# Four of six block inverses: formed in place in SBUF instead of PSUM, on two engines instead of one

## The chip, the cores and the metric

The kernel runs on one core of a Trainium2 chip. A core has TensorE (PE in the profile; PEld is its weight load), VectorE (DVE), ScalarE (ACT), GpSimd (POOL) and SyncE (SP, which here only issues DMAs). The metric is the device time of one execution in microseconds, the median of several.

## The reference, cut to what matters

A DeltaNet attention block (4 batches, 8 heads, 768 tokens, 48 features) followed by a multiplicative feed-forward block on 3072 tokens:

```
state = 0
for t in range(768):
    y[t] = q[t] @ state
    state += beta[t] * outer(k_n[t], v[t] - state.T @ k_n[t])      # k_n: k divided by its norm
x = y, heads beside each other                                      # (3072, 384)
out = ((x @ w1) * (x @ w2) @ w3) @ w_out                            # d_ff = 1024
```

## The kernel before, in words

The recurrence is cut into 12 chunks of 64 tokens. Within a chunk it becomes a triangular system: with a strictly upper matrix U of scores, the kernel needs the inverse of (1 + U). U is cut into 32 x 32 blocks; the two diagonal blocks are inverted directly, and the off-diagonal corner follows from two products. Two chunks are inverted together: 2 chunks x 2 block places x 32 (batch, head) pairs = 128 blocks, one per partition, with the 32 x 32 elements of a block in the free dimension. So there are six inverses, j = 0 to 5, and inverse j serves the chunks 2j and 2j + 1.

The steps of one inverse are the generator `inverse(j)`, whose name in the list of steps is `Vj`. V0 and V1 (`TURNED`) come from SBUF by transposes and are not changed. For V2 to V5 the blocks go through DRAM: `to_blocks` (u) writes them to `Ud`, L503 loads them into the SBUF tile `Ub` (U in the code), and ScalarE writes the identity into V, a pair of PSUM banks taken with `two_banks()` (L509, L514). Then come 31 dependent steps of two VectorE instructions: a product of a column of V and a row of U into the SBUF tile `tb` (L534), and its subtraction from V in PSUM (L539). Two ScalarE copies (L548) bring V back to SBUF, and L552 stores it to `Vd`; `from_blocks` reads it from there as the first step of `corner` (e). While V is in work its pair of banks is held; the psW pool has two such pairs, so everything else that uses `two_banks()` (scores s, corner e, chain c, outputs y) takes turns on the other one.

The other parts that matter here, by their names in the list: `c` is the chain of three products per chunk that carries the state, `y` its outputs, `n` a scaling of v on GpSimd (L666), `g` and `N` squares and norms of k (L329, L345 to L358), `d` transposes on VectorE (L383), `s` scores with a mask on GpSimd (L452). In the feed-forward part the tokens come in six groups u of 512. For u = 1 to 5 the hidden layer is formed by `m` (`pair`), 20 additions of products on TensorE (L1091) per half with their evictions on ScalarE and VectorE, after sums of tokens (`G`) and of weights (`W`, `T`); then come sums of the results (`S`) and the last products `o` (L1263) with their results `x` (L1293). The elementwise sums and products of G, W, S and of three steps of m go through one helper (L200):

```
def alone(out, x, y, op):
    (dve if other else pool).tensor_tensor(out=out, in0=x, in1=y, op=op)
```

The order of all work is written out by hand: `ORDER` is a text of some 1700 names, and each name runs the next step of its generator. All instructions of one engine run in the order of this text. A mark (') behind a name sets `other`, so that `alone` takes VectorE instead of GpSimd, and `put` changes sides between ScalarE and VectorE.

Of the kernel before, what the change touches and what calls it, by code (L numbers as in the profile page):

```python
# [51 lines left out]
P35 P29 v2 V1 V1 y1 b3 b1 y1 P28 y1 P29 f6 b2 c1 P29 f6 P34 b1 V1 V1 V1 V1 P31 P27 P28 V1 V1 V1 a00
f6 b2 P34 a02 a02 a00 P27 P28 V1 d4 P35 V1 V1 d4 a01 P34 a01 V1 V1 V1 V1 V1 V1 P35 a04 P31 P33 v3
a04 P33 a05 a03 a03 a05 b7 b7 a06 b5 p4 k4 n3 n2 n2 P35 V1 P30 V1 V1 V1 e2 P32 c1 a06 P33 d4 P31 k5
b4 a07 c2 d4 e2 e2 b4 e3 e2 b5 e2 P33 a04 e3 e3 a07 e2 c2 p5 b4 e2 a05 e2 P30 P32 c2 e3 P31 g2 g2 g2
g2 g2 a05 P30 b6 b6 b4 c2 y2 g2 g2 g2 P32 g2 a07 d5 d5 P30 p5 P32 b2 c2 N2 W n3 y2 s4 c2 b0 s4 a04
k6 T a07 s4 T s4 s4 b2 s4 e3 W s4 e3 a00 N2 a02 b0 d5 a00 d5 s5 s5 s5 s5 s5 s5 u4 a01 a01 S0' u5 V2
a06 s5 a02 p6 v4 c3 e3 g3 T W W T b1 W b6 W W W g3 a06 c3 b1 b5 b5 b6 S0 V2 e3 c3 c3 V2 V2 V2 V2 V2
V2 V2 V2 V2 a03 a03 b3 y3 b7 b3 y3 V2 b7 S0 W d6 V2 V2 V2 y3 W V2 V2 oA0 S0 S0 S0 V2 V2 oD0 S0 S0
S0' V2 n4 oB0 W W S0 S0 S0 xA0 oA0 c3 xA0 xB0 V2 d6 G1' W G1 oB0 c3 c4 xA0 oC0 V2 V2 V2 V2 V2 xB0 V2  # L60
m10 W W m10 S0 xD0 S0' G1 G1 G1 m10 m10 m10 m10 m10 G1' m10 p6 v5 S0 n4 W W xC0 V2 V2 V2 V2 V2 xC0
xD0 S0' V2 V2 V2 W' m10 V2 V2 e4 oC0 m10 m10 m10 d6 xC0 G1' c4 G1 W G1' m10 m10 m10 m10 m10 m10 m10
m10 m10 m10 m10 m10 m10 k7 s4 G1' G1' W' m10 e4 m10 m10 m10 m10' m10 m10 e4 e4 m10 e4 m10 m10 m10 e4
xC0 d6 p7 m10 m10 m10 m10 m10 m10 m10 m11 c4 n5 g3 c4 G1 g3 s5 m10 g3 g3 g3 m10 g3 m11 m10 m10' g3
m11 y4 d7 m11 m11 m11 m11 m11 d7 m11 N3 e5 m11 s6 m11 m11 m11 m11 m11 m11 m11 y4 p7 s6 s6 e5 m11 m11
m11 m11 d7 m11 c4 c4 d7 e5 e5 m11 m11 m11 m11 s6 k8 v6 s7 s7 s7 m11 g4 s7 s7 s7 m11 m11 s7 s6 n5 s6
m11 m11 g4 m11 m11 u7 u6 s6 m11 c5 e5 m11 c5 V3 m11 m11 m11 e5 V3 m11 m11 m11 m11 m11 c5 m11 oA1 c5
p8 S1' g4 g4 m11 V3 m11 S1 S1 y5 xA1 y5 N3 V3 V3 V3 V3 V3 V3 V3 d8 m11 V3 y5 oD1 d8 S1 S1 S1 V3 V3
V3 oB1 V3 V3 oA1 xB1 xA1 v7 n6 V3 V3 V3 V3 V3 G2 S1 n7 xA1 p8 S1 G2 G2 G2 c5 k9 G2 oB1 V3 V3 xB1 xD1
oC1 V3 m20 m20 m20 m20 m20 m20 m20 G2 m20 V3 xC1 xC1 V3 V3 V3 V3 m20 oC1 m20 m20 V3 V3 V3 V3 V3 xD1  # L70
G2 G2' xC1 m20 m20 m20 m20 m20 m20 s6 G2' m20 m20 m20 m20 m20 g4 s7 G2' n6 V3 V3 V3 c5 e6 xC1 m20
m20 m20 m20 m20 m20 m20 m20 m20 m20 m20 m20 c6 m20 c6 G2 G2 e6 m20 m20 m20 m20 e6 m20 g4 m20 m20 m20
m21 e6 e6 e7 d8 g4 e6 g4 g4 m21 m20 d8 m20 m21 c6 c6 s8 N4 s8 m20 m20 m21 m21 m21 m21 m21 m21 y6 p9
d9 d9 p9 s8 m21 m21 m21 m21 m21 m21 c6 y6 e7 m21 m21 m21 s8 m21 m21 c6 m21 s8 m21 s8 e7 d9 d9 m21 e7
m21 s8 m21 m21 m21' m21 s9 s9 m21 m21 n7 s9 s9 S2 s9 s9 m21 m21 u8 m21 m21 c7 m21 v8 m21 N4 m21 c7
s9 u9 V4 m21 m21 m21 m21 e7 e7 m21 m21 c7 c7 m21 m21 m21' S2 oA2 y7 oD2 S2 n8 S2 V4 V4 V4 V4 V4 V4
V4 V4 xA2 v9 V4 V4 V4 oB2 V4 V4 p10 d10 V4 S2 m21 n9 S2 xB2 oA2 V4 d10 y7 y7 oB2 V4 V4 V4 V4 G3 G3
G3 G3 G3 xB2 V4 V4 c7 xA2 p10 oC2 xA2 xD2 G3 m30 m30 m30 m30 m30 V4 V4 V4 V4 V4 xC2 n8 S2 G3 xC2 k10
S2 V4 V4 G3 G3 G3' V4 xD2 g5 s8 m30 m30 m30 m30 oC2 V4 V4 xC2 V4 V4 xC2 m30 m30 m30 m30 m30 m30 m30
m30 m30 m30 m30 m30 m30 V4 V4 c7 V4 m30 m30 m30 d10 m30 m30 m30 k11 m30 g5 G3 g5 m30 m30 e8 m30 m30  # L80
m30 c8 m30 m30 m31 g5 e8 c8 e8 m30 m30 m31 e8 m30 G3 m30 m30 e8 m30 n9 e9 e8 d10 s9 g5 g5 g5 g5 p11
m31 c8 m30 e9 m30 c8 y8 m30 e9 g5 e9 m30 N5 m30 m31 m31 m31 m31 m31 m31 m31 m31 d11 s10 d11 s10 p11
m31 m31 N5 m31 m31 s10 m31 m31 m31 m31 m31 m31 m31 c8 c8 y8 s10 s10 s10 s10 e9 m31 m31 m31 d11 d11
m31 e9 s11 s11 s11 s11 s11 s11 m31 m31 m31 m31 m31 m31 m31 m31 S3 c9 m31 c9 m31 m31 m31 m31 m31 m31
m31 s11 m31 u10 u11 V5 c9 c9 m31 V5 V5 y9 y9 y9 V5 V5 V5 oA3 m31 m31 S3 S3 oD3 S3 S3 m31 xA3 G4 V5
V5 V5 V5 V5 V5 V5 V5 V5 V5 G4 oB3 S3 oA3 S3 V5 V5 V5 V5 oC3 V5 xB3 V5 V5 V5 G4 G4 G4' V5 oB3 S3 xA3
xB3 xA3 G4 xD3 G4 G4 c9 V5 m40 m40 m40 m40 m40 m40 m40 m40 xC3 V5 V5 V5 V5 m40 V5 V5 m40 V5 V5 xC3
V5 V5 xD3 v10 n10 G4' oC3 c9 xC3 G4 V5 e10 v11 m40 m40 m40 m40 m40 m40 m40 m40 m40 m40 m40 m40 m40
m40 m40 m40 m40 m40 m40 s11 n10 m40 m40 m40 m40 G4 e10 c10 s10 e10 m40 m40 m40 G4 c10 m40 e10 m40
m40 m40 m40 m40 m40 e10 m41 m40 m41 m41 m41 e10 c10 e11 e11 m40 m40' m40' m41 m41 m41 m41 c10 c10  # L90
m41 e11 m41 m41 m41 c10 e11 m41 m41 m41 m41 m41 m41 m41 m41 m41 m41 m41 m41 m41 m41 m41 m41 m41 m41
n11 m41 m41 m41 m41 e11 c11 e11 m41 m41 m41 m41 m41 n11 c11 m41 m41 m41 c11 c11 y10 m41 m41 oA4 xA4
y10 y11 y11 m41 S4' m41' m41 S4' S4 S4 oD4 oB4 xB4 S4 oA4 S4 S4 oB4 xA4 y11 oC4 xB4 S4 G5' G5' G5 G5
xA4 xC3 xD4 xC4 xC4 G5' G5 m50 xD4 m50 m50 m50 m50 m50 m50 m50 m50 m50 m50 oC4 xC4 xC4 G5 G5' G5 G5
G5 G5 m50 m50 m50 m50 m50 m50 m50 m50 m50 m50 m50 m50 m50 m50 m50 m50 m50 m50 m50 m50 m50 m50 m50
m50 m50 m50 m50 m50 m50 m50 m50 m50 m51 m50 m50 m50' m50' m51 m51 m51 m51 m51 m51 m51 m51 m51 m51
m51 m51 m51 m51 m51 m51 m51 m51 m51 m51 m51 m51 m51 m51 m51 m51 m51 m51 m51 m51 m51 m51 m51 m51 m51
# [6 lines left out]
def kernel(  # L104
# [94 lines left out]
    def alone(out, x, y, op):  # L199
        (dve if other else pool).tensor_tensor(out=out, in0=x, in1=y, op=op)  # L200
# [297 lines left out]
    def inverse(j):  # L498
        U = in_turn(work, [P, BS, BS], "Ub", 1, "Ub")
        if j in TURNED:  # L500
            dve.transpose(out=U[:], in_=columns().rearrange("p t m g -> p t (m g)"))
# [7 lines left out]
        act.copy(  # L509
            out=flat[:, 0:n].rearrange("p (s t) -> p s t", t=BS + 1),  # L510
            in_=eye[:, 0 : BS + 1].unsqueeze(1).to_broadcast([P, BS - 1, BS + 1]),
# [948 lines left out]
```

## Time and profile before

| | |
|---|---|
| median of 3 runs | 568.31 us (566.58 to 569.11) |
| the profiled execution, its own time | 571.55 us |
| its span in the profile | 569.5 us |
| TensorE busy | 522.2 us |
| VectorE busy | 412.1 us |
| GpSimd busy | 269.6 us |
| ScalarE busy | 225.7 us |
| mean granted TensorE clock | 0.981 |

A row of groups in the profile reads: line, engine, operation, output <- inputs, shapes, count | busy us, mean ns of one | idle time of the engine just before, and what ended it. A row of the timeline reads: start in us, duration in us, engine, line, operation, shapes, count of merged instructions. A row of stretches reads: the stretch and its length, then the busy time of PE, PEld, DVE, ACT and POOL with the number of instructions in brackets, the granted clock, and the DMA share and rate. A row of waits reads: who waited, for whom, us in total, times, the longest.

### The profile page before, as it was taken

Reading aid. Unit: us, or ns where it says so; the run is one execution under the profiler, and the core shown is the slowest. Engines: PE = TensorE matmul, PEld = TensorE weight load, DVE = VectorE, ACT = ScalarE, POOL = GpSimd, SP = SyncE. Lnnn points to the kernel's source line nnn. Section 1 sums busy time; section 2 is a strip of 40 time slices with the busy share of each in tenths; the row PEclk is TensorE's granted clock in tenths of the full one; section 3 lists DMA queues with packets and bytes.
Section 4 is the critical chain, followed back from the end, with each engine's and each line's share of the span. In section 5 each row is a group of like instructions: output and inputs, shape, how many; then the busy total and the mean of one; then the engine's idle time right before and its main releaser. Section 6 shows DMA issues by size and latency. Waiting matters only on the chain.

```text
span 569.5 us, 19879 instructions
## 1 busy us (share of the span) xinstructions
PE 522.2 (92%) x8460; PEld 433.0 (76%) x8460; DVE 412.1 (72%) x881; ACT 225.7 (40%) x461; POOL 269.6 (47%) x287
## 2 busy tenths in 40 slices
...
GB/s 224 257 131 217 206 178 116 159 149 145 67 58 105 29 84 108 77 81 92 90 87 83 52 122 67 95 115 52 79 29 64 118 13 2 16 61 9 0 2 55
DMA packets 197591, 52.63 MB, mean 92 GB/s; under 512 B 184576, under 2 KB 191872, under 8 KB 197504
## 3 DMA queue, kind: packets, MB, share of 16 engines
...
q8 instruction: 66, 1.08, 0.8%
...
## 4 chain that ended last, share of the span: by engine, by line
PE 61%; DVE 20%; DMA 6%; issue 4%; SPq 3%; ACT 2%; POOL 1%; DVEq 0%; ACTq 0%; POOLq 0%
PE ps_f L1091 29%; PE ps_f L1263 13%; PE ps_w L680 4%; DMA raw<-in_moe_w_dram 3%; PE ps_w L779 3%; DVE tb L534 3%; PE ps_f L908 3%; DVE ps_w L539 2%; PE ps_w L609 2%; DVE ps_w L528 2%; DVE tb L523 2%; PE ps_w L432 2%; PE ps_w L426 2%; DVE ab L200 1%; DVE KQ L383 1%
## 5 line engine op out<-in xcount | busy, mean ns | idle before, releaser
L200 POOL TENSOR_TENSOR ab<-ab 128x512 f32<-128x512 f32 (+1 forms) x56 | 64.2, 1158 | 107.8 <-DVE ab L1170 66.4
L1263 PE MATMUL ps_f<-w,ab 128*128 128x192 f32 x376 | 65.3, 327 | 0.9 <-DVE ab L200 0.9
L1091 PE MATMUL ps_f<-xT,w1s 128*128 128x256 f32 x240 | 62.1, 390 | 2.6 <-DVE ab L1111 2.0
L1263 PEld LDWEIGHTS ps_f<-w,ab 128*128 128x128 f32 x376 | 61.8, 190 | 1.9 <-DVE ab L200 1.2
L1091 PE MATMUL ps_f<-xT,w2s 128*128 128x256 f32 x240 | 61.3, 388 | 1.6 <-DVE x_room L1108 0.7
L1108 DVE TENSOR_TENSOR ab<-ab,ps_f 128x512 f32<-128x512 f32 x60 | 41.0, 683 | 21.2 <-PE ps_f L1091 19.0
L1091 PEld LDWEIGHTS ps_f<-xT,w1s 128*128 128x128 f32 x240 | 42.6, 189 | 12.7 <-DVE ab L1108 2.5
L1091 PEld LDWEIGHTS ps_f<-xT,w2s 128*128 128x128 f32 x240 | 43.7, 190 | 10.7 <-issue 2.0
L1263 PE MATMUL ps_f<-room,ab 128*128 128x192 f32 x272 | 47.2, 329 | 4.0 <-DVE room L1293 2.8
L888 PE MATMUL ps_f<-w2s,w3T 128*128 128x384 f32 x128 | 45.9, 507 | 3.6 <-POOL w2s L837 3.0
L1263 PEld LDWEIGHTS ps_f<-room,ab 128*128 128x128 f32 x272 | 44.2, 190 | 5.1 <-DVE room L1293 2.4
L452 POOL TENSOR_TENSOR PT<-PT,smask 128x512 f32<-128x512 f32 x20 | 25.6, 1278 | 45.5 <-ACT PT L450 45.4
L539 DVE TENSOR_TENSOR ps_w<-ps_w,tb 128x31 f32<-128x31 f32 (+15 forms) x124 | 43.3, 349 | 4.5
L534 DVE TENSOR_TENSOR tb<-ps_w,Ub 128x31 f32<-128x31 f32 (+15 forms) x124 | 41.9, 338 | 4.8 <-DMA Ub<-Ud 1.7
L1091 PE MATMUL ps_f<-xT,room 128*128 128x256 f32 x160 | 41.7, 388 | 1.9 <-DVE osb L1293 1.9
L1102 ACT COPY ab<-ps_f 128x512 f32<-128x512 f32 x20 | 11.7, 585 | 72.9 <-PE ps_f L1091 67.5
L888 PEld LDWEIGHTS ps_f<-w2s,w3T 128*128 128x128 f32 x128 | 24.2, 196 | 19.9 <-POOL w2s L837 4.2
L798 ACT COPY xT<-ps_w 48x256 f32<-48x256 f32 x96 | 30.4, 365 | 16.6 <-PE ps_w L779 15.8
L1091 PEld LDWEIGHTS ps_f<-xT,room 128*128 128x128 f32 x160 | 29.0, 190 | 8.4 <-POOL xT L200 2.6
L426 PE MATMUL ps_w<-KQ 48*64 48x128 f32 x384 | 29.6, 299 | 5.5 <-DVE S L742 4.4
L432 PE MATMUL ps_w<-KQ 48*64 48x64 f32 x768 | 30.3, 235 | 2.9 <-issue 2.9
L1108 DVE TENSOR_TENSOR x_room<-x_room,ps_f 128x512 f32<-128x512 f32 x40 | 27.3, 683 | 6.6 <-PE ps_f L1091 5.9
...
## 6 DMA issues: line engine op xcount, KB each, us to landing
...
```

What stands on the lines that cost most here:

```text
L200: (dve if other else pool).tensor_tensor(out=out, in0=x, in1=y, op=op)
L426: pe.matmul(ps[half(z), 0, n : n + 128], lhsT=x[:, 0, :], rhs=x.rearrange("p j t -> p (j t)"), start=True, stop=True,)
L432: pe.matmul(ps[half(z ^ j), 1, n + C * j : n + C * j + C], lhsT=x[:, 0, :], rhs=x[:, j, :], start=True, stop=True,)
L452: pool.tensor_tensor(out=PT, in0=PT, in1=smask[:].unsqueeze(1).to_broadcast([P, H, C]), op=ALU.mult)
L534: dve.tensor_tensor(out=tv, in0=V[:, 0 : s + 1, s : s + 1].to_broadcast([P, s + 1, n]), in1=U[:, s, s + 1 : BS].unsqueeze(1).to_broadcast( ...
L539: dve.tensor_tensor(out=o, in0=o, in1=tv, op=ALU.subtract)
L680: pe.matmul(out(ps, r, h, z), lhsT=lhs(r, h, z), rhs=rhs(r, h, z), start=True, stop=True,)
L798: act.copy(out=xT[f, cc, p:NP:2, b : b + NR, :].rearrange("p a r t -> p r a t"), in_=pyv[f, z, b : b + NR],)
L888: pe.matmul(ps[:, 0:DM], lhsT=w3Ts[jc, kc // 4][:, kc % 4 * P : kc % 4 * P + P], rhs=wo[:, kc], start=(i == 0), stop=(i == KF - 1),)
L1091: pe.matmul(ps[:, n * g : n * g + n].rearrange("p (b c t) -> p b c t", b=HB, c=2), lhsT=product_weights(i, 2 * r + g), rhs=of[i], start=ne ...
L1108: dve.tensor_tensor(out=t, in0=t, in1=cell(name), op=ALU.add)
L1263: pe.matmul(ps[b][:, b, :], lhsT=block(u, HF * f + i, z)[:, P * b : P * b + P], rhs=ws_[w][:, i], start=first and i == 0 and (b == 0 or n ...
```

## The change

For j in 2 to 5 the inverse is formed in place in the SBUF tile `Ub`. ScalarE changes the sign of the whole tile, GpSimd sets everything on and below the diagonal to zero (`affine_select`), ScalarE writes ones on the diagonal. Then 30 steps follow, each with two instructions through `alone`: the product of a column and a row of U into `tb`, and its addition to U. No bank of PSUM is taken or held, and the tile is stored to `Vd` as it is.

```
+    ON_CHIP = (2, 3, 4, 5,)
...
+        if j in ON_CHIP:
+            flat = U[:].rearrange("p s t -> p (s t)")
+            act.mul(out=flat, in_=flat, mul=-1.0)
+            yield
+            pool.affine_select(
+                out=U[:], in_=U[:], pattern=[[-1, BS], [1, BS]], compare_op=ALU.is_gt,
+                fill=0.0, base=0, channel_multiplier=0,
+            )
+            yield
+            act.copy(
+                out=flat[:, 0 : BS * BS : BS + 1], in_=eye[:, 0:1].to_broadcast([P, BS])
+            )
+            yield
+            for s in range(1, BS - 1):
+                n = BS - 1 - s
+                t = in_turn(work, [P, 256], "tb", 2, "tb")
+                tv = t[:, 0 : s * n].rearrange("p (r t) -> p r t", t=n)
+                alone(
+                    tv, U[:, 0:s, s : s + 1].to_broadcast([P, s, n]),
+                    U[:, s, s + 1 : BS].unsqueeze(1).to_broadcast([P, s, n]), ALU.mult,
+                )
+                o = U[:, 0:s, s + 1 : BS]
+                alone(o, o, tv, ALU.add)
+                yield
+            Vds[j] = in_turn(dram, [P, BS, BS], "Vd", 2, "Vd")
+            sync.dma_start(out=Vds[j][:], in_=U[:])
+            yield
+            return
```

`ORDER` is new from its tenth line on (the start, up to about the first transposes of w3, is as before). Each of V2 to V5 has 35 names instead of 37. The marks that put a step on VectorE, counted over the whole list:

| steps | marked before | marked after |
|---|---|---|
| V2, V3, V4, V5 (30 arithmetic steps each) | (always VectorE) | 26, 25, 25, 22 |
| S, all groups | 14 | 28 |
| G, all groups | 16 | 27 |
| W | 2 | 10 |
| m, all | 11 | 15 |
| f4, t12 | 0, 0 | 1, 1 |

As an example of how the steps lie, the new list around V3:

```
m11 c5 m11 m11 m11 c5 oA1 m11 m11 c5 V3 xA1 g4 m11 g4 V3 v7 p8 V3 g4 m11' V3' V3' V3' V3' S1 V3' V3'
V3' V3' V3' V3' V3' V3' V3' V3' V3' c5 y5 m11 c5 oD1 y5 oA1 S1 S1 oB1 xB1 S1 S1 n6 oC1 y5 V3 d8 V3'
V3' V3' d8 G2 xA1 oB1 k9 xA1 G2' xB1 G2' G2' xD1 xC1 m20 S1' n6 S1 G2' V3 G2 V3 G2' c6 m20 m20 m20
m20 p8 m20 m20 m20 V3' V3' V3' V3' V3' V3' xC1 G2' G2 V3 m20 V3' V3 V3 xD1 oC1 e6 g4 m20 m20 m20
```

More of the change, by code (lines that the diff above doesn't have):

```diff
@@ L52 @@
[L52 to L97, printed above, removed]
@@ new lines @@
+t13 y1 b3 P28 P28 V1 V1 V1 V1 V1 V1 V1 y1 f6 P34 P30 b0 f6 f6 P28 c1 b0 P30 P33 b7 V1 V1 y1 p4 b2 b2
+b7 a05 a06 P30 V1 V1 V1 P33 a06 a05 V1 c1 a03 V1 V1 P34 P35 a04 b6 P33 a03 d4 P34 V1 V1 P30 P34 b6
+a04 P35 d4 V1 P35 P31 P31 P35 V1 V1 P31 V1 V1 V1 V1 V1 a00 c2 P32 a01 b4 v2 a02 N1 a01 a02 P31 b4
+P32 P32 b5 a00 b5 n2 b4 a06 P32 b1 V1 e2 e2 e2 k4 n2 g2 b4 e2 b3 e2 p4 e3 c2 a00 g2 g2 g2 a06 e2 e2
+e2 a02 d4 b3 b1 d4 W W' W' c2 b0 b2 k5 c2 b0 c2 b2 e3 g2 g2 g2 W e3 v3 p5 y2 g2 c2 e3 a00 a02 g2 y2
@@ new lines @@
+s4 b6 a01 a05 a04 d5 d5 N2 s4 s4 T N2 T T n3 W' s4 k6 e3 b6 s4 a01 n3 g3 a05 W' W a07 b7 p5 v4 W' e3
+s4 s4 d5 d5 c3 c3 n4 s5 s5 s5 a07 s5 n4 s5 a04 e3 e3 s5 b5 W W' b7 u4 u5 V2 s5 a07 c3 V2 p6 a03 a07
+W b5 c3 a03 T S0' S0' S0' W' W' S0' y3 y3 y3 W' g3 oA0 oD0 xA0 V2 S0' S0' V2 V2' V2 d6 S0' V2' c3
+S0' S0' S0' S0' V2 V2' V2' V2' S0 V2 oB0 c3 xB0 V2' V2' V2' oA0 xA0 k7 oB0 G1' V2' V2' S0 V2' xA0 v5
+G1' oC0 V2' xB0 G1 G1 s4 S0 G1 G1' xD0 S0' d6 m10 m10 m10 m10 m10 m10 m10 V2 V2' xC0 W V2' xC0 W'
@@ new lines @@
+V2' V2' V2' m10 m10 V2' G1' V2' G1' m10 S0 W V2' V2' V2' V2' V2' V2' V2' oC0 xD0 m10 m10 m10 m10 m10
+m10 m10 xC0 m10 W W W s5 G1 m10 m10 m10 m10 m10 m10 g3 G1 G1 p6 V2 m10 d6 m10 xC0 m10 m10 G1 n5 m10
+m10 m10 m10 g3 g3 m10 m10 e4 c4 m10 m10 m10 e4 c4 m10 d6 m10 m10 g3 g3 e4 e4 m10 m10 m10 m11 e4 m10
+m10 g3 e4 g3 m11 m11 c4 c4 p7 N3 m11 y4 m10 n5 m10 m11 m11 m11 m11 d7 d7 e5 p7 c4 k8 v6 m11 m11 m11
+m11 m11 m11 m11 m11 m11 e5 c4 m11 m11 m11 m11 m11 N3 y4 s6 s6 s6 e5 m11 d7 d7 m11 e5 m11 s7 s7 m11
@@ new lines @@
+s7 s7 s7 s7 s7 s6 m11 m11 m11 g4 s6 s6 u7 u6 V3 m11' m11 m11 m11 m11 S1' s6 e5 e5 c5 m11 m11 m11 m11
+m11 c5 m11 m11 m11 c5 oA1 m11 m11 c5 V3 xA1 g4 m11 g4 V3 v7 p8 V3 g4 m11' V3' V3' V3' V3' S1 V3' V3'
+V3' V3' V3' V3' V3' V3' V3' V3' V3' c5 y5 m11 c5 oD1 y5 oA1 S1 S1 oB1 xB1 S1 S1 n6 oC1 y5 V3 d8 V3'
+V3' V3' d8 G2 xA1 oB1 k9 xA1 G2' xB1 G2' G2' xD1 xC1 m20 S1' n6 S1 G2' V3 G2 V3 G2' c6 m20 m20 m20
+m20 p8 m20 m20 m20 V3' V3' V3' V3' V3' V3' xC1 G2' G2 V3 m20 V3' V3 V3 xD1 oC1 e6 g4 m20 m20 m20 xC1
@@ new lines @@
+c7 oA2 p10 V4 xA2 S2' m21 m21 m21' S2' S2' S2' y7 y7 g5 V4 V4 V4 g5 V4' V4' v8 V4' V4' y7 c7 s9 g5
+V4' oB2 oD2 v9 g5 c7 V4 m21' V4 xB2 V4' d10 d10 oA2 V4' V4' V4' V4' V4' xA2 S2 S2 V4' oB2 k11 xA2
+oC2 xB2 xD2 G3 G3' m30 m30 G3 G3 G3 G3 m30 m30 p10 m30 n8 xC2 xC2 xD2 V4' V4' V4' m30 V4' G3 S2 m30
+m30 m30 V4' G3' G3' c8 S2 m30 m30 m30 m30 N4 m30 m30 V4' V4' V4' V4' G3 m30 V4' V4' V4' oC2 g5 V4'
+n9 V4 g5 g5 V4 xC2 m30 m30 m30 m30 m30 n8 G3 m30 m30 m30 m30 c8 G3' n9 V4 m30 m30 m30 m30 m30 m30
+m30 m30 m30 m30 m30 m30 m30 m30 m31 e8 m31 d10 d10 m30 e8 m30 g5 g5 m30 m30 e8 e8 m31 m30 m30 e8 e8
@@ new lines @@
+m31 s10 N5 s10 c8 m30 m30 m31 s10 s10 c8 p11 m31 m31 m31 m31 m31 e9 s10 s10 s10 y8 d11 d11 p11 m31
+m31 e9 m31 v10 m31 xC2 u10 m31 y8 e9 m31 m31 m31 m31 m31 m31 m31 c8 c8 d11 e9 e9 e9 d11 m31 m31 m31
+m31 m31 m31 m31 c9 s11 s10 m31 c9 s11 s11 s11 m31 m31 m31 m31 s11 s11 u11 V5 c9 m31 m31 m31 N5 s11
+m31 m31 m31 m31 m31 c9 m31 oA3 S3' m31 m31 m31' S3' y9 V5 y9 y9 S3 S3 m31' oD3 xA3 oB3 V5 V5 V5' V5'
+V5' V5' V5' oA3 s11 S3' S3 xB3 oB3 V5' V5' V5' V5' V5' V5' V5' xB3 xA3 v11 xA3 oC3 S3' S3 G4 G4' G4'
```

28 lines of the change are left out of this document (22 added, 6 removed).

## Prediction

> **What bounds the kernel now.** I read the page first: busy shares, then the chain that ended last.
>
> ```profile
> span 569.5 us, 19879 instructions
> PE 522.2 (92%) x8460; PEld 433.0 (76%) x8460; DVE 412.1 (72%) x881; ACT 225.7 (40%) x461; POOL 269.6 (47%) x287
> PE 61%; DVE 20%; DMA 6%; issue 4%; SPq 3%; ACT 2%; POOL 1%; DVEq 0%; ACTq 0%; POOLq 0%
> ```
>
> TensorE (PE) is idle for 569.5 - 522.2 = 47.3 us in all, and the change removes no matmul. A gain can only come out of those 47 us, and only out of the part that lies where the four changed inverses lie. So the second view is the table by stretches. The first four run from the first step of V2, V3, V4 and V5 to the first product of the corner that needs the result; the other four from the first to the last step of each.
>
> ```profile
> core 0: us, PE busy (x) PEld busy (x) DVE busy (x) ACT busy (x) POOL busy (x), PEclk, DMA share, GB/s
> 178.70:224.60 45.90, 40.77 (x450) 35.26 (x452) 42.66 (x95) 8.67 (x19) 32.34 (x39) 1.00 0.35 71
> 266.20:304.70 38.50, 36.80 (x396) 31.70 (x385) 34.21 (x85) 9.88 (x23) 24.14 (x25) 1.00 0.42 85
> 341.00:379.50 38.50, 38.38 (x445) 33.58 (x447) 34.62 (x87) 9.77 (x22) 25.71 (x28) 1.00 0.51 98
> 415.20:456.80 41.60, 41.48 (x522) 36.55 (x525) 34.67 (x86) 10.84 (x23) 24.31 (x25) 1.00 0.30 68
> 178.70:213.20 34.50, 30.34 (x399) 27.55 (x398) 32.61 (x79) 5.40 (x14) 28.92 (x36) 1.00 0.31 60
> 266.20:293.30 27.10, 25.39 (x286) 23.27 (x275) 24.70 (x70) 6.55 (x17) 20.22 (x21) 1.00 0.45 83
> 341.00:368.20 27.20, 27.08 (x327) 25.34 (x327) 25.09 (x72) 6.72 (x16) 18.59 (x20) 1.00 0.45 78
> 415.20:442.50 27.30, 27.18 (x330) 25.53 (x330) 24.76 (x71) 6.01 (x15) 16.29 (x16) 1.00 0.18 46
> ```
>
> Two things are to be seen. PE's idle time in the four long stretches is 5.1 + 1.7 + 0.1 + 0.1 = 7.0 us: that is all a better inverse can win there. And while an inverse runs, VectorE (DVE) is busy 91 to 95% of the time: it is as full as PE, and a few microseconds more on it make PE wait.
>
> **The arithmetic steps.** The old steps of V2 to V5 are these groups.
>
> ```profile
> L539 DVE TENSOR_TENSOR ps_w<-ps_w,tb 128x31 f32<-128x31 f32 (+15 forms) x124 | 43.3, 349 | 4.5
> L534 DVE TENSOR_TENSOR tb<-ps_w,Ub 128x31 f32<-128x31 f32 (+15 forms) x124 | 41.9, 338 | 4.8 <-DMA Ub<-Ud 1.7
> L539 DVE TENSOR_TENSOR ps_w<-ps_w,tb 128x255 f32<-128x255 f32 x8 | 3.5, 432 | 0.3
> L539 DVE TENSOR_TENSOR ps_w<-ps_w,tb 128x31 f32<-128x31 f32 x8 | 1.6, 199 | 0.6
> L200 DVE TENSOR_TENSOR ab<-ab 128x512 f32<-128x512 f32 x16 | 10.5, 688 | 1.5 <-PE ps_f L1263 1.3
> L200 POOL TENSOR_TENSOR ab<-ab 128x512 f32<-128x512 f32 x44 | 55.8, 1277 | 107.8 <-DVE ab L1170 66.4 <-DVE ab L1108 18.5 <-DVE ab L200 16.8
> L200 POOL TENSOR_TENSOR xT<-xT 128x256 f32<-128x256 f32 x36 | 26.2, 738 | 11.0 <-DVE xT L200 8.2 <-DMA xT<-xT 2.3
> ```
>
> DVE pays (432 - 199) / 224 = 1.04 ns per element and about 0.16 us per instruction, and 688 ns for 512 elements wholly in SBUF is on that line, so SBUF operands by themselves cost DVE nothing. GpSimd (POOL) pays (1277 - 738) / 256 = 2.1 ns per element and 0.2 us per instruction; below 256 elements this is an estimate from those two rows. An old inverse has 5456 elements in each of its two passes, a new one 4960 (s(31-s) for s = 1 to 30).
>
> In the new list a mark behind a step's name puts it on DVE. Of the 30 steps of V2, V3, V4 and V5, 26, 25, 25 and 22 are marked. On DVE: 196 instructions and 34,028 elements, 196 x 0.16 + 34.0 x 1.04 = 66.7 us, where 43.3 + 41.9 = 85.2 us go. On POOL: 44 instructions and 5,652 elements, 8.8 + 11.9 = 20.7 us. The steps depend on each other, so what counts for one inverse is the sum: about 21.9 us against 21.3. The chain gets no shorter.
>
> **Head and tail.** Three rows price them.
>
> ```profile
> L509 ACT COPY ps_w<-eye 128x1023 f32<-128x1023 f32 x6 | 6.1, 1024 | 6.0 <-DVE vtok L711 3.6 <-DVE X L720 2.3
> L548 ACT COPY Ub<-ps_w 128x512 f32<-128x512 f32 x8 | 4.3, 591 | 4.6 <-DVE ps_w L539 4.6
> 1.81 0.29 POOL L215 TENSOR_SCALAR_AFFINE_SELECT strict<-strict 128x128 f32<-128x128 f32 x1
> ```
>
> The identity written into PSUM (1.02 us on ScalarE) went beside the load; in its place the chain gets a sign change (1.0), a select of 1024 elements, and a small copy of the diagonal (some 0.2). The select is between 0.3 us (its own 128 elements) and 8 x 0.29 = 2.3; I take 1.3. The tail loses two copies, 1.2 us. Net +1.3 us per inverse, on ScalarE and POOL, which have room at the start; I count it at nothing where the load comes early, else 5 us for the four.
>
> **What else the list moves.** Steps of the slab sums, token sums, weight sums and products go from POOL to DVE: marks on S 14 to 28, G 16 to 27, W 2 to 10, m 11 to 15. On DVE that is 14 + 11 + 8 + 4 instructions, 19 of 256 elements at 0.41 and 18 of 512 at 0.69, plus two copies: 21.6 us. POOL loses 19 x 0.73 + 18 x 1.28 = 36.9. Without anything else DVE would come to 412.1 - 85.2 + 66.7 + 21.6 = 415 us, POOL to 270 + 21 + 5 - 37 = 259. Busy time hardly changes.
>
> **The cost that decides: two engines and one way into SBUF.** An old step has one operand in PSUM. A new one on DVE has both in SBUF. What such an instruction meets when POOL works shows in the timeline.
>
> ```profile
> 217.22 0.41 DVE L200 TENSOR_TENSOR xT<-xT 128x256 f32<-128x256 f32 x1
> 192.20 4.56 DVE L200 TENSOR_TENSOR ab<-ab 128x256 f32<-128x256 f32 x1
> 191.65 1.40 POOL L200 TENSOR_TENSOR room<-room,w1s 128x256 f32<-128x256 f32 x2
> 193.02 2.08 POOL L200 TENSOR_TENSOR ab<-ab 128x256 f32<-128x256 f32 x3
> 195.07 1.40 POOL L200 TENSOR_TENSOR w2s<-room,w2s 128x256 f32<-128x256 f32 x2
> 240.92 0.19 DVE L348 TENSOR_TENSOR nt<-nt,nr 128x32 f32<-128x32 f32 x1
> 151.57 0.93 DVE L348 TENSOR_TENSOR nt<-nt,seed 128x32 f32<-128x32 f32 x1
> 151.45 1.96 POOL L958 TENSOR_TENSOR room<-w 128x384 f32<-128x384 f32 x2
> ```
>
> The same 256 elements take 0.41 us alone and 4.56 us while POOL has a row of instructions: DVE ends when POOL's queue runs dry at 196.47. A 0.19 us instruction takes 0.93 beside POOL, one POOL instruction's length. In the same stretch the old steps of V2, with PSUM operands, keep their 0.4 us. The Trainium skill's page "SBUF — State Buffer" (§ SBUF: two separate sides) says that a VectorE instruction with two SBUF inputs and a GpSimd instruction that reads SBUF exclude each other, and that the loser blocks until the first is through. The rows agree, with one addition: 4.56 us spans several POOL instructions, so the loser can lose again.
>
> How much POOL work do the 196 instructions meet? Between the first and the last step of each inverse the new list has on POOL, its own V steps left out: for V2 four S0, three G1, two W, one s4, 8.9 us; for V3 six S1, one m11, three G2, two n6, 12.8; for V4 four S2, seven G3, three g5, two n, one s9, 15.6; for V5 two S3, six G4, two n10, one s11, 9.8; in all 47 us (n, g and s by the rows below).
>
> ```profile
> L666 POOL TENSOR_TENSOR vtok<-vtok,n 128x384 f32<-128x384 f32 x24 | 20.5, 863 | 16.0 <-DMA vtok<-in_v_dram 16.0
> L329 POOL TENSOR_TENSOR sq<-ktok 128x384 f32<-128x384 f32 x24 | 19.8, 832 | 23.8 <-DMA out_dram<-osb 12.5 <-DVE ss L331 4.5 <-DMA ktok<-in_k_dram 3.7
> L452 POOL TENSOR_TENSOR PT<-PT,smask 128x512 f32<-128x512 f32 x20 | 25.6, 1278 | 45.5 <-ACT PT L450 45.4
> ```
>
> The bounds are 0 (every POOL instruction falls while DVE reads PSUM or waits) and 47 (each stops DVE for its whole length). DVE's own time there is 70 to 80% SBUF-only, and for about a quarter of the chain the step is on POOL and DVE isn't stopped. 0.78 x 0.77 gives 0.6: 28 us, 7 per inverse.
>
> **What of it reaches the end.** PE goes on until the corner's product. By the two lists, PE's work from an inverse's first step to that product is 40.8, 34.6, 32.0 and 35.4 us before, and 32.0, 34.9, 36.5 and 33.1 after, summed with these durations (one addition of a product is four records, 0.93 us):
>
> ```profile
> 291.49 10.24 PE ps_f L1091 x44
> 288.89 2.60 PE ps_f L1263 x16
> 301.74 1.08 PE ps_w L680 x64
> 304.74 0.69 PE ps_w L609 x50
> ```
>
> DVE needs, between first and last step, its V steps, marked sums and five to nine other instructions, 27.3, 24.9, 26.6 and 21.7 us. With 3.9, 5.1, 3.8 and 7.1 us of V steps on POOL and 0.6 of the POOL work above, 36.5, 37.7, 39.8 and 34.7; the trace before has 34.5, 27.1, 27.2 and 27.3. From the last step to the product it takes 11.4, 11.4, 11.3 and 14.3 us before; I take 11. Against PE's work in the list, and 0, 2, 6 and 6 us by which PE did more than the list's share before, PE lacks 15.5, 11.8, 8 and 6.6 us, where it lacked 5.1, 1.7, 0.1 and 0.1: +35 us. This is too much, since DVE's other instructions (5.2, 5.2, 7.5 and 3.6 us) can run while POOL has a V step; the smaller of the two, inverse by inverse, is 3.9 + 5.1 + 3.8 + 3.6 = 16 us. That leaves +19. The pair of PSUM banks that V no longer holds gives the score, corner and chain products a second place; it can win back only idle time that is already in the 7 us, and the larger waits above take that away, so I count it at nothing.
>
> Sum: the profiled execution took 571.55 us (span 569.5); it would take 590.5. The median of the runs before, 568.31, is 3.2 lower, so I predict 587.
>
> **The rivals.** First, the waits hardly coincide, because POOL is idle for half of the time and its work slips to where DVE reads PSUM. Then the sum without blocking counts, 35 - 28 - 16 = -9, and PE's idle 7 us in the four stretches go, with the second PSUM place to help: 568.3 - 7 = 561. For it speaks that the list takes 37 us off POOL, and that V3' stands eleven times in a row with no POOL step between; against it that these rows are list order, not time. It decides if less than a fifth of the 47 us blocks. Second, full exclusion: all 47 us block, 0.4 x 47 = 19 more: +38, 606. A row of POOL instructions as at 191.65 speaks for it, the many gaps of POOL against it; it decides where POOL always has work when DVE reaches a step. The skill's rule named above, taken without a gap, is this case. Third, the 22 POOL steps stand in a queue that waits for DVE:
>
> ```profile
> POOL ab L200 <- DVE ab L1170: 66.4, 8, 18.9
> ```
>
> If one V step in each inverse lands behind such a wait of mean 66.4 / 8 = 8.3 us, that is +33 us, 601. The list puts those products mostly behind the inverse, which speaks against it. Fourth, blocked time and new room cancel: no change beyond 0.5% (2.8 us, about what a measurement of this kernel can tell from none).
>
> **How the numbers follow.** The forecast has 0.54; the first rival 0.22 (its gain is 7 us at most, so nearly all of it lies beyond 0.5%); full exclusion 0.10; the queue 0.07; no change 0.07. Slower: 0.54 + 0.10 + 0.07 = 0.71. The range goes from the first rival's 561, a little below, to full exclusion's 606: 560 to 606. The forecast's own range is 575 to 600.
>
> **What would show it.** Right: the new add and multiply on DVE average well over 0.34 us, with single ones of 1 us and more that end when a POOL instruction ends; DVE's busy time rises to 440 or more; PE's idle time in the four stretches goes from 7 to about 25 us, ended by the corner's inputs or by DVE. What would make it wrong: DVE's V steps keep 0.34 us on average, or they are stretched and PE stays busy all the same, because PE's order leaves more work between than I counted.

## Result and the profile after

The changed kernel takes 605.59 us (median of 4 runs, 602.73 to 608.57); the kernel before took 567.96 us (566.58 to 569.11) beside it. The ratio is 1.0664, 95% interval 1.0588 to 1.074: 37.6 us slower.

The page of the changed kernel, and two views by groups: the steps of V2 to V5 on DVE and on POOL.

```profile
span 606.7 us, 19888 instructions
PE 533.7 (88%) x8460; PEld 440.6 (73%) x8460; DVE 447.2 (74%) x872; ACT 221.1 (36%) x451; POOL 264.9 (44%) x294
```

```profile
L201 DVE TENSOR_TENSOR tb<-Ub 128x130 f32<-128x130 f32 (+14 forms) x98 | 49.2, 502 | 9.0 <-POOL Ub L511 4.0
L201 DVE TENSOR_TENSOR Ub<-Ub,tb 128x130 f32<-128x130 f32 (+14 forms) x98 | 48.5, 495 | 3.7 <-ACT Ub L516 0.2
```

```profile
L201 POOL TENSOR_TENSOR Ub<-Ub,tb 128x30 f32<-128x30 f32 (+11 forms) x22 | 11.4, 516 | 1.7
L201 POOL TENSOR_TENSOR tb<-Ub 128x30 f32<-128x30 f32 (+11 forms) x22 | 9.8, 444 | 41.9 <-DVE Ub L201 41.4
```

PE has the same 8460 matmuls. Its idle time rose from 47.3 to 606.7 - 533.7 = 73.0 us, and the same matmuls took 533.7 us instead of 522.2: 25.7 + 11.5 = 37.2 us, the whole loss between the two profiled executions. The mean granted clock fell from 0.981 to 0.961, which is about the same 2% by which the matmuls got longer. The 196 steps on DVE take 97.7 us; worked out without blocking they were 66.7. POOL's 44 take 21.2.

The stretches of the changed kernel, as in the prediction: four from the first step of an inverse to the first product of the corner, four from the first step to the last.

```profile
core 0: us, PE busy (x) PEld busy (x) DVE busy (x) ACT busy (x) POOL busy (x), PEclk, DMA share, GB/s
181.30:232.30 51.00, 39.78 (x295) 33.40 (x293) 45.98 (x89) 7.38 (x16) 26.89 (x32) 0.90 0.30 63
274.60:318.90 44.30, 35.08 (x228) 30.58 (x228) 40.96 (x78) 7.77 (x18) 23.00 (x27) 0.88 0.33 65
357.00:409.90 52.90, 44.19 (x442) 36.99 (x441) 46.59 (x88) 10.04 (x24) 26.58 (x32) 0.94 0.33 66
451.80:495.20 43.40, 37.99 (x296) 31.66 (x294) 37.47 (x72) 6.78 (x13) 22.43 (x32) 0.96 0.21 54
181.30:220.40 39.10, 28.54 (x195) 24.77 (x193) 36.99 (x75) 5.61 (x13) 22.06 (x26) 0.91 0.28 53
274.60:309.90 35.30, 26.08 (x187) 24.14 (x187) 33.60 (x67) 5.99 (x15) 18.10 (x22) 0.85 0.26 45
357.00:399.00 42.00, 34.16 (x401) 29.31 (x401) 38.28 (x75) 7.68 (x20) 21.83 (x28) 0.95 0.31 59
451.80:486.70 34.90, 30.30 (x205) 25.62 (x203) 31.11 (x63) 5.01 (x10) 17.60 (x28) 0.95 0.15 40
```

The four long stretches last 191.6 us, where they lasted 164.5, and PE is idle in them for 11.2 + 9.2 + 8.7 + 5.4 = 34.6 us (unrounded), where it was idle for 7.0. DVE is still busy about 90% of the time, and PE is busy for 157.0 us in them as before (157.4): the stretches got longer, and PE didn't get more to do. The clock column, 1.00 in all four before, is now 0.88 to 0.96.

One place shows the mechanism: V3's first steps in the timeline, DVE, then POOL, then PE.

```profile
274.60 1.24 DVE L201 TENSOR_TENSOR tb<-Ub 128x30 f32<-128x30 f32 x1 [1.61 <-POOL Ub L511]
275.88 1.19 DVE L201 TENSOR_TENSOR Ub<-Ub,tb 128x30 f32<-128x30 f32 x1
...
282.89 0.27 DVE L201 TENSOR_TENSOR Ub<-Ub,tb 128x108 f32<-128x108 f32 x1
...
292.78 0.55 DVE L1323 TENSOR_TENSOR room<-room,ps_f 128x384 f32<-128x384 f32 x1
```

```profile
274.53 1.27 POOL L201 TENSOR_TENSOR ab<-ab 128x512 f32<-128x512 f32 x1
275.76 1.27 POOL L201 TENSOR_TENSOR ab<-x_room,late 128x512 f32<-128x512 f32 x1
276.98 4.96 POOL L201 TENSOR_TENSOR ab<-ab 128x512 f32<-128x512 f32 x4
281.90 0.83 POOL L696 TENSOR_TENSOR vtok<-vtok,n 128x384 f32<-128x384 f32 x1
```

```profile
282.25 2.76 PE L1293 MATMUL ps_f<-w,ab 128*128 128x192 f32 x16
293.48 5.46 PE L1293 MATMUL ps_f<-room,ab 128*128 128x192 f32 x16 [8.47 <-POOL Ub L201]
```

POOL runs six slab sums and a token scaling without a gap, and DVE ends one V step per POOL instruction. From 282.9 a step of 108 elements takes 0.27 us. Behind the run of V steps stands L1323, which empties the PSUM bank that PE needs: PE waits 8.47 us. The releaser printed there (what ended the wait, by the profile) is a V step on POOL that ends at 293.43; PE reads nothing of it, and L1323 ends at 293.33. After the pause, 16 matmuls take 5.46 us where the 16 ahead of it took 2.76. PE's waits by line name the same kind of place elsewhere, an eviction (L1323) that stands in DVE's order behind other work:

```profile
PE ps_f L1121 <- DVE osb L1323: 10.0, 4, 4.2
PE ps_f L1293 <- POOL Ub L201: 8.5, 1, 8.5
```

### The profile page after: what moved, and what is told of

Read it like the earlier page. It is cut to its first block, busy times and chain, and to the rows that moved or that the text cites. A ratio compares the mean times of both kernels' runs of the same rounds, so it can differ in the third digit from the quotient of the medians.

```text
span 606.7 us, 19888 instructions
## 1 busy us (share of the span) xinstructions
PE 533.7 (88%) x8460; PEld 440.6 (73%) x8460; DVE 447.2 (74%) x872; ACT 221.1 (36%) x451; POOL 264.9 (44%) x294
## 5 line engine op out<-in xcount | busy, mean ns | idle before, releaser
L201 POOL TENSOR_TENSOR ab<-ab 128x512 f32<-128x512 f32 (+1 forms) x39 | 49.3, 1271 | 122.4 <-DVE ab L1200 76.4
L1121 PE MATMUL ps_f<-xT,w1s 128*128 128x256 f32 x240 | 66.2, 409 | 12.9 <-ACT ps_f L1166 6.0
L1293 PE MATMUL ps_f<-w,ab 128*128 128x192 f32 x376 | 65.3, 327 | 0.0
L1121 PE MATMUL ps_f<-xT,w2s 128*128 128x256 f32 x240 | 63.8, 400 | 0.9 <-DVE x_room L1138 0.5
L1121 PEld LDWEIGHTS ps_f<-xT,w1s 128*128 128x128 f32 x240 | 45.2, 199 | 25.9 <-ACT ps_f L1166 7.9
L1293 PEld LDWEIGHTS ps_f<-w,ab 128*128 128x128 f32 x376 | 61.8, 190 | 0.9 <-DVE ab L201 0.3
L1293 PE MATMUL ps_f<-room,ab 128*128 128x192 f32 x272 | 51.0, 343 | 11.9 <-POOL Ub L201 8.5
L1293 PEld LDWEIGHTS ps_f<-room,ab 128*128 128x128 f32 x272 | 46.4, 198 | 14.6 <-POOL Ub L201 8.7
L201 DVE TENSOR_TENSOR tb<-Ub 128x130 f32<-128x130 f32 (+14 forms) x98 | 49.2, 502 | 9.0 <-POOL Ub L511 4.0
L1121 PE MATMUL ps_f<-xT,room 128*128 128x256 f32 x160 | 45.0, 412 | 10.6 <-DVE osb L1323 6.9
L1121 PEld LDWEIGHTS ps_f<-xT,w2s 128*128 128x128 f32 x240 | 46.6, 200 | 9.9 <-ACT x_room L1132 1.5
L201 DVE TENSOR_TENSOR Ub<-Ub,tb 128x130 f32<-128x130 f32 (+14 forms) x98 | 48.5, 495 | 3.7 <-ACT Ub L516 0.2
L1132 ACT COPY ab<-ps_f 128x512 f32<-128x512 f32 x20 | 11.7, 586 | 97.7 <-PE ps_f L1121 97.5
L453 POOL TENSOR_TENSOR PT<-PT,smask 128x512 f32<-128x512 f32 x20 | 26.0, 1300 | 47.5 <-ACT PT L451 47.5
L828 ACT COPY xT<-ps_w 48x256 f32<-48x256 f32 x96 | 30.5, 366 | 11.0 <-PE ps_w L809 10.5
```

Source lines behind the costliest of these rows:

```text
L453: pool.tensor_tensor(out=PT, in0=PT, in1=smask[:].unsqueeze(1).to_broadcast([P, H, C]), op=ALU.mult)
L828: act.copy(out=xT[f, cc, p:NP:2, b : b + NR, :].rearrange("p a r t -> p r a t"), in_=pyv[f, z, b : b + NR],)
L1121: pe.matmul(ps[:, n * g : n * g + n].rearrange("p (b c t) -> p b c t", b=HB, c=2), lhsT=product_weights(i, 2 * r + g), rhs=of[i], start=ne ...
L1132: act.copy(out=t, in_=cell(name))
L1293: pe.matmul(ps[b][:, b, :], lhsT=block(u, HF * f + i, z)[:, P * b : P * b + P], rhs=ws_[w][:, i], start=first and i == 0 and (b == 0 or n ...
```

## Experiments

Every ratio is taken to the kernel before, run beside it on the same chip. These runs come from three chips, on which the kernel before took 570.12, 569.99 and 568.04 us; beside the changed kernel it took 567.96. A difference in us between two runs below can therefore be off by some 2 us.

**The old arithmetic in the new list.** All 31 steps in PSUM on DVE, with the pair of banks held again; the list of steps is the new one.

```
         if j in ON_CHIP:
-            flat = U[:].rearrange("p s t -> p (s t)")      # ... sign, select, ones,
-            for s in range(1, BS - 1):                     # ... 30 steps in U
+            V = two_banks().rearrange("p a (s t) -> p (a s) t", t=BS)
+            held.add(("w", turns["w"]))
+            ...                                            # the old identity, 31 steps, two copies
+            held.clear()
```

> The new list of steps with the old arithmetic: V2 to V5 are formed in a held pair of PSUM banks, all 31 steps on VectorE whatever their mark; everything else as in the changed kernel. Theory (the steps are slow because both operands are in SBUF beside GpSimd): their 248 VectorE instructions go back to about 0.34 us, 85 us in all, PE's idle time in the stretches beside the inverses falls by 15 us or more, and the time is 575 to 588 us. Rival (the new list itself is what costs: evictions that PE waits for stand behind long runs of V steps, and VectorE has more sums to do): 597 us or more, since VectorE has even more to do here.

```profile
L528 DVE TENSOR_TENSOR ps_w<-ps_w,tb 128x31 f32<-128x31 f32 (+15 forms) x124 | 43.3, 349 | 8.7 <-ACT ps_w L517 4.4
L523 DVE TENSOR_TENSOR tb<-ps_w,Ub 128x31 f32<-128x31 f32 (+15 forms) x124 | 41.9, 338 | 3.8 <-DMA Ub<-Ud 0.8
```

615.16 us, ratio 1.0794 (1.073 to 1.0858). The steps took their old 0.34 us beside the same POOL work, as the theory said, but the time was above both kernels. The theory took the held pair to cost nothing, and that is what fell. One wait of PE is the largest of all here:

```profile
PE ps_w L811 <- DVE S L774: 14.6, 1, 14.6
```

This run mixes the operands' place, the list and the held pair, so it does not rule out the rival, that the list costs, whose 597 us or more it meets. The third run below has the pair alone.

**The new arithmetic in the old list.** The new branch goes into the kernel before, with all 30 steps on DVE and the old `ORDER`.

```
-                alone(
+                dve.tensor_tensor(
...
-                alone(o, o, tv, ALU.add)
+                dve.tensor_tensor(out=o, in0=o, in1=tv, op=ALU.add)
```

> The old list of steps with the new arithmetic: V2 to V5 in place in SBUF, all 30 steps on VectorE; sums stay on GpSimd as in the kernel before. Theory (two SBUF operands beside GpSimd): 240 VectorE instructions that alone would take 80 us take 115 to 130 us (mean 0.48 to 0.54), and the time is 595 to 612 us. Rival (the new list costs, the place of the operands doesn't): mean 0.33 us and 566 to 575 us.

```profile
L523 DVE TENSOR_TENSOR tb<-Ub 128x30 f32<-128x30 f32 (+14 forms) x120 | 63.4, 529 | 17.0 <-POOL Ub L510 14.0
L528 DVE TENSOR_TENSOR Ub<-Ub,tb 128x30 f32<-128x30 f32 (+14 forms) x120 | 61.7, 514 | 7.1 <-ACT Ub L515 2.8
...
PE ps_f L1292 <- DVE room L1322: 33.0, 4, 11.2
```

626.19 us, 1.0993 (1.0946 to 1.1039). With the list unchanged, the new arithmetic takes the steps from 85.2 to 125.1 us, within the theory's 115 to 130, and the kernel is 56 us slower, more than the theory's bound of 612 allows. PE's largest wait is again for an eviction on DVE. The operands' place is not all that differs: the new head comes with it, and the first steps wait 14.0 us for its select (L510, the first row above), which has its place in GpSimd's order. How the 56 us divide is not shown. The new list wins back about 20 us of them; by which of its moves is not shown either.

**The held pair, alone.** The changed kernel takes and holds an unused pair during each inverse.

```
+            unused = two_banks()
+            act.copy(out=unused[:, 0, 0:32], in_=eye[:, 0:32])
+            held.add(("w", turns["w"]))
             for s in range(1, BS - 1):
...
+            act.copy(out=U[:, 0, 0:1], in_=unused[:, 0, 0:1])
+            held.clear()
```

> The changed kernel, but V2 to V5 take a pair of PSUM banks that they don't use and hold it until they are stored, as the kernel before did; two small copies on ScalarE per inverse are added. Theory (the second pair wins nothing that counts): within 3 us of the changed kernel. Rival (the freed pair is worth something, and the blocking costs more than the net change shows): slower than the changed kernel by 5 us or more.

```profile
292.17 1.11 PE L814 MATMUL ps_w<-KQ,S 48*48 48x64 f32 x32 [16.54 <-DVE S L777]
```

620.78 us, 1.0899 (1.0839 to 1.0959): 13 us (by the ratios) to 15 us above the changed kernel, where the theory allowed 3. One wait is as large as that: the outputs y5 need the one pair that is left, and the DVE instruction that reads it (S) stands in the queue behind V3's run. The old arithmetic in the new list had the same wait (14.6 us). So the new list does lean on the freed pair. Against this run, the old arithmetic in the new list is 5.6 us cheaper, with 124 steps on DVE where this one has 98. While the pair is held, then, the place of the operands makes little difference to the whole: PE waits for the pair instead.

**The held pair in the old list.** The same hold, added to the second experiment.

> The old list with the steps in place on VectorE, as before, but V2 to V5 hold a pair of PSUM banks that they don't use. Theory (the pair is worth something only to a list that was made for it): 623 to 630 us, as without the held pair (626). Rival (a second pair is worth 10 us or more in any list): 636 us or more.

626.01 us, 1.0984 (1.0954 to 1.1013), against 626.19: in the old list the freed pair is worth nothing. Of these two orders, only the new one uses it.

**POOL only writes.** While an inverse is in work, the unmarked sums of S, G, W and m on POOL become memsets of about the same length; V's own steps stay. It leaves those sums out.

```
     def alone(out, x, y, op):
+        if running_v and not own and not other:
+            w = out.shape[-1]
+            pool.memset(out, 0.0)
+            pool.memset(out, 0.0)
+            pool.memset(out[..., 0 : w // 4], 0.0)
+            return
```

> The changed kernel, in which the sums that GpSimd does between the first and the last step of V2 to V5 (S, G, W, m without a mark) are replaced by memsets of about the same length into the same tiles, so these sums are left out of the result. GpSimd is as busy and gates the same products, but reads nothing from SBUF. Theory (GpSimd's reads stop VectorE's second operand): V steps on VectorE fall from a mean of 0.50 to 0.34 to 0.39 us, the time to 575 to 590 us. Rival A (any GpSimd instruction stops them, or they are slow for another reason): mean 0.46 us or more, time 598 or more. Rival B (the steps get faster, but PE waits in line for other things all the same): mean under 0.40 us, time 598 or more.

```profile
L209 DVE TENSOR_TENSOR tb<-Ub 128x130 f32<-128x130 f32 (+14 forms) x98 | 39.2, 400 | 6.7 <-POOL Ub L519 2.4 <-POOL Ub L209 1.9
L209 DVE TENSOR_TENSOR Ub<-Ub,tb 128x130 f32<-128x130 f32 (+14 forms) x98 | 38.4, 391 | 3.7
```

587.9 us, 1.0302 (1.0247 to 1.0357). The steps fell from 97.7 to 77.6 us (mean 0.395, a hair above the theory's 0.39), and the kernel won some 18 us.

**POOL only writes, everywhere.** The squares (L330), the score mask (L453) and the scaling of v (L696) become memsets too.

```
+                if running_v:
+                    in_place_of(sq[:], False)
+                else:
                     pool.tensor_tensor(out=sq[:], in0=kt[:, r], in1=kt[:, r], op=ALU.mult)
```

> As the run with writes only, and now GpSimd's scalings of v, squares of k and score masks beside an inverse are also memsets of about their length, so all of GpSimd's work between first and last step of V2 to V5, the V steps apart, reads nothing; these results are left out. Theory: V steps on VectorE come down to what they take alone, a mean of 0.34 to 0.36 us, and the time to 578 to 586 us; what then remains over the kernel before, 8 to 16 us, is not blocking but the new list: evictions that PE needs stand behind runs of V steps, and PE's clock falls after its pauses. Rival: blocking was all of it: 575 us or less.

The page, the groups, the four long stretches, and the same two V3 steps beside POOL's memsets:

```profile
PE 520.6 (90%) x8460; PEld 431.2 (75%) x8460; DVE 417.7 (72%) x872; ACT 220.5 (38%) x451; POOL 260.6 (45%) x385
...
L213 DVE TENSOR_TENSOR Ub<-Ub,tb 128x130 f32<-128x130 f32 (+14 forms) x98 | 36.0, 367 | 4.3 <-ACT Ub L534 0.7
L213 DVE TENSOR_TENSOR tb<-Ub 128x130 f32<-128x130 f32 (+14 forms) x98 | 35.4, 361 | 8.6 <-POOL Ub L529 3.7 <-POOL Ub L213 2.5
```

```profile
182.30:227.60 45.30, 37.87 (x295) 32.27 (x294) 40.38 (x89) 7.36 (x16) 25.95 (x53) 0.92 0.33 70
269.10:304.90 35.80, 32.65 (x242) 28.01 (x233) 32.38 (x78) 7.80 (x18) 22.34 (x50) 1.00 0.41 80
343.60:387.60 44.00, 40.19 (x436) 34.15 (x434) 39.01 (x88) 9.92 (x24) 24.68 (x61) 1.00 0.39 79
429.70:467.20 37.50, 35.86 (x297) 30.60 (x295) 31.66 (x72) 6.80 (x13) 21.32 (x52) 1.00 0.25 63
```

```profile
269.18 0.19 DVE L213 TENSOR_TENSOR tb<-Ub 128x30 f32<-128x30 f32 x1 [1.31 <-POOL Ub L529]
269.40 0.19 DVE L213 TENSOR_TENSOR Ub<-Ub,tb 128x30 f32<-128x30 f32 x1
...
269.08 0.53 POOL L204 MEMSET ab<- 128x512 f32 x1
```

579.31 us, 1.0166 (1.0135 to 1.0198). POOL is as busy as before (260.6 against 264.9 us), the list is the same, and the steps take 0.364 us on average. The two steps that took 1.24 and 1.19 us beside POOL's sums take 0.19 beside its memsets. So POOL's reading is what stops them. The kernel's 26 us need not all be blocking, though: a memset has no inputs to wait for, so POOL can also start sooner than with the sum in whose place it stands. The Trainium skill's page "SBUF — State Buffer" (§ Who interferes with whom) has it that a VectorE instruction with two SBUF inputs contends with a GpSimd instruction that reads SBUF, and not with one that only writes; this run agrees.

It also says where most of the 37.6 us are. In the four long stretches, 162.6 us now stand against 191.6. PE's idle time in them fell from 34.6 to 16.0, its busy time from 157.0 to 146.6: 18.6 + 10.5 = 29 us, the difference of the two spans but for 1 us (606.7 - 578.7 = 28.0). What is left is 9.3 us over the kernel before. PE's idle time in the stretches is 16.0 where it was 7.0, so this rest lies in the same place: I put it down to the list, in which evictions stand behind runs of V steps. That is argued from the stretches, not shown by a run of its own; POOL's own V steps, which still read, are in it too.

**A pause filled.** Eight dummy matmuls (16 records in the profile) before the second oB1 of V3, into a pair of banks of their own, so that PE works through the 8.5 us pause.

```
-V3' V3' d8 G2 xA1 oB1 k9 ...
+V3' V3' d8 G2 xA1 oB1+8 k9 ...
...
+            if unread[0]:
+                skip("w")
+                fill(two_banks()[:, 0])
```

> The changed kernel with eight matmuls on the identity, whose result nothing reads, put ahead of the second half of oB1, where PE paused 8.5 us and then took 5.46 us for 16 records that take 2.60 elsewhere. Theory (PE's clock falls in a pause and comes back after some microseconds of work): these 16 records take 2.6 to 3.3 us, and PE's real work is shorter by 2 to 3 us; the time falls by no more than that, which is about the spread of the runs. Rival (the records are slow because other engines load the memories at that moment): 4.5 us or more as before.

```profile
285.40 7.03 PE L195 MATMUL ps_w<-ident 128*128 128x512 f32 x16
292.31 2.84 PE L1296 MATMUL ps_f<-room,ab 128*128 128x192 f32 x16
...
299.50 1.13 PE L1121 MATMUL ps_f<-xT,room 128*128 128x256 f32 x4 [2.42 <-DVE osb L1326]
```

609.27 us, 1.0681 (1.0644 to 1.0718). The matmuls after the pause took 2.84 us instead of 5.46: the idling ahead of them had made them slow. The 2.6 us went into the next wait for an eviction on DVE (2.42 us), and the time did not fall. The Trainium skill's page "TensorE: Matmul & The Clock Gate" (Part 1) has the array at half its clock after an idle window of some 3.4 us, until it has been busy for as long; the time here, 5.46 us against 2.84, agrees. But the 2.6 us at this place were not to be had back by keeping PE busy: the slow matmuls filled time in which PE would have waited. Whether that holds for all of the 11.5 us of slower matmuls is not shown.

**All steps on GpSimd.** The opposite end: in V2 to V5 every `V'` of the new list becomes `V`.

```
-... V3 g4 m11' V3' V3' V3' V3' S1 V3' V3'
+... V3 g4 m11' V3 V3 V3 V3 S1 V3 V3
```

> The changed kernel with no mark on V2 to V5, so all 120 steps are on GpSimd and VectorE does none of them. Theory (the end is set by the length of an inverse, first step to last, with what stands between on its engine): 240 instructions at 0.18 us and 2.1 ns per element, 43 + 83 = 126 us on GpSimd, with 47 us of its other work between: 43 us per inverse where the changed kernel has 37, so 620 to 640 us. Rival (blocked VectorE evictions are what PE waits for, not the inverse): VectorE is free of V and PE waits less, 600 us or less.

```profile
L201 POOL TENSOR_TENSOR Ub<-Ub,tb 128x30 f32<-128x30 f32 (+14 forms) x120 | 63.5, 529 | 12.3 <-ACT Ub L516 3.0
L201 POOL TENSOR_TENSOR tb<-Ub 128x30 f32<-128x30 f32 (+14 forms) x120 | 61.9, 516 | 7.6
...
PE ps_f L1293 <- POOL ab L201: 32.3, 5, 14.4
```

650.91 us, 1.1445 (1.1391 to 1.1499). The steps take 125.4 us, as worked out from POOL's rows; the time is 11 us above the theory's range. The slab sums that PE needs now queue behind V on POOL (32.3 us of waits). POOL is no way out.

**The same blocking in the kernel before.** The prediction's row of 4.56 us is a marked S0 sum. In the old list three marks of S0 and two of G1 that lie in V2 or just beside it are taken away, so that these sums go to POOL; nothing else is changed.

```
-S0' V2 n4 oB0 W W S0 S0 S0 xA0 ...  m10 W W m10 S0 xD0 S0' G1 G1 G1 m10 m10 m10 m10 m10 G1' m10 ...
+S0 V2 n4 oB0 W W S0 S0 S0 xA0 ...   m10 W W m10 S0 xD0 S0 G1 G1 G1 m10 m10 m10 m10 m10 G1 m10 ...
```

> The kernel before, with the marks taken off three S0 and two G1 steps that VectorE did in 0.85 to 4.56 us each beside GpSimd (0.41 alone); they go to GpSimd, 0.72 us each. Theory (VectorE bounds the stretch of V2 and is rid of some 6.5 us of blocked time, GpSimd gets 3.6 us more): faster than the kernel before by 1 to 4 us. Rival (GpSimd's sums are themselves what the products wait for there): the same or up to 4 us slower.

The timeline of PE in the kernel before, then the same matmuls here:

```profile
198.07 2.87 PE L1263 MATMUL ps_f<-room,ab 128*128 128x192 f32 x16 [2.28 <-DVE room L1293]
```

```profile
194.12 2.87 PE L1263 MATMUL ps_f<-room,ab 128*128 128x192 f32 x16
```

565.76 us, 0.9937 (0.9908 to 0.9966): 2 to 5 us faster than the kernel before. DVE is no longer stopped ahead of the eviction L1293, and PE's wait for it is gone. Five sums less on DVE would be a relief of 5 x 0.41 = 2.1 us without any blocking, so how much of the gain is the blocking is not settled. One blocked sum remained, so one more mark was taken away:

```
-S0 V2 n4 oB0 ... xB0 V2 d6 G1' W G1 oB0 c3 ...
+S0 V2 n4 oB0 ... xB0 V2 d6 G1 W G1 oB0 c3 ...
```

> The kernel before without the five marks taken off in the last run, and without the first G1 mark too, the one step that still lost 2.5 us (2.96 instead of 0.41) beside GpSimd in that run. Theory (each blocked step on the path of the stretch of V2 costs what it is blocked): 1 to 3 us under that run, 562 to 565 us. Rival (GpSimd, busy 34 of 37 us there, bounds that stretch by now): no gain or up to 2 us back.

564.97 us, 0.9935 (0.991 to 0.9961): no further gain by the ratios, so here the rival came true. These two, which can't be told apart, are the only versions here that beat both kernels.

## Why the prediction was right or wrong

**Right: sign and mechanism; too small: the size.** The forecast was 587 us, with a range of its own of 575 to 600. Measured is 605.59: 37.6 us more than before, where 19 were forecast. Of the whole range it meets the upper end, 606, which was set by the second rival. The cost that decides is the one named. The steps average 0.50 us where 0.34 was the reference, single ones of over 1 us end with a POOL instruction, and DVE is busy 447 us (440 or more was asked). Blocking measures 97.7 - 66.7 = 31 us where 0.6 of 47 us gave 28 (26 against the 71.4 that the steps took with POOL's reads gone). Both factors are a little off: POOL's work beside the inverses is some 58 us (79.6 busy in the four shorter stretches, less 21.2 of V), and about half of it blocks. With POOL's reads beside the inverses gone, 605.6 falls to 579.3.

**The term that was too small: what DVE has to do beside the steps.** The prediction added up the inverses to 36.5, 37.7, 39.8 and 34.7 us, 148.7 in all, then took 16 us off because DVE's other instructions can run while POOL has a V step. That is how +35 became +19. Measured are 39.1, 35.3, 42.0 and 34.9, 151.3 in all, as if nothing had been taken off. But the overlap is there: from the start of POOL's V steps to their ends, 23.2 us in all, DVE is busy for 18.9. One place in V3:

```profile
298.15 0.59 POOL L201 TENSOR_TENSOR tb<-Ub 128x220 f32<-128x220 f32 x1 [1.70 <-DVE Ub L201]
298.81 0.67 POOL L201 TENSOR_TENSOR Ub<-Ub,tb 128x220 f32<-128x220 f32 x1
...
298.55 0.47 DVE L201 TENSOR_TENSOR xT<-xT,xT 128x256 f32<-128x256 f32 x1
298.97 0.55 DVE L1323 TENSOR_TENSOR room<-room,ps_f 128x384 f32<-128x384 f32 x1
```

What came out larger is DVE's own work. In the four shorter stretches it is busy for 140.0 us, where the sum had 100.5 and 28 of blocking. The V steps are little of this (97.7 against 66.7 + 28). The rest are DVE's other instructions, some 42 us where the sum had 34: beside the marked sums there are 9 to 16 of them in an inverse, not five to nine. And DVE is idle for 11.3 us, where the sum left 4; about 6 of them are gaps of under 0.1 us from one instruction to the next, which the sum did not have. POOL's V steps (20.7 worked out, 21.2 measured) held.

So the sum without the deduction, 571.55 + 35 - 3.2 = 603, comes near the measured 605.6 by luck: it leaves out an overlap of about the size of the work that was left out as well.

**A term that was missing.** PE's idle time in the four stretches was to go from 7 to about 25 us; it went to 34.6. Outside them it fell a little, so that it rose by 25.7 us in all. The other 11.5 us of the loss are the same matmuls at a lower granted clock, which the prediction did not have. How much of these 11.5 us is a loss of its own, and how much only fills a wait as at the one place that was tried, is not shown.

**The path was another one.** PE was to go on until the corner's product and wait there for the inverse. It didn't: after all four inverses the first product of the corner follows the matmuls before it without a wait, as here after V3:

```profile
318.87 0.76 PE L639 MATMUL ps_w<-T,U 33*33 33x32 f32 x64
```

All of the 34.6 us lie earlier. 27 of them end with an instruction of DVE, 19 with the eviction L1323 (V3's 8.47 counted with it), which stands behind V steps and marked sums in DVE's order. A chain of blocked steps delays whatever is queued behind it, and here its own result came in time. So the sum of an inverse's length and 11 us says how long DVE's work takes, but not what PE waits for.

**"Counted at nothing": right by half.** In the old list the freed pair is worth nothing. But without it the new list would cost 13 to 15 us more, so its price depends on the order. The rest of 9 us, put down to the list above, was no term of its own in the prediction.

**The rivals.** No blocking (561) fell with the first view of the steps. Full exclusion (606) has nearly the measured time, but not its reason: 31 us blocked, not all of the 47 that the list gave or the 58 that the trace has. That its number came out is luck. The POOL steps behind a wait for DVE did show up, as POOL's wait for V:

```profile
POOL tb L201 <- DVE Ub L201: 41.4, 13, 9.4
```

That is POOL waiting for its turn in V's own chain, not V waiting behind a product on POOL, which was the rival.
